# Four result tiles stored with one transfer each instead of two, and the last copy shared by two engines

## The chip, the cores and the metric

The kernel runs on one core of a Trainium2 chip. A core has a matrix engine (TensorE, PE in the profile), two engines that can read its accumulators in PSUM (VectorE, DVE in the profile, and ScalarE, ACT), GpSimd (POOL), and SyncE (SP), which here issues nearly all transfers between the chip's memory (HBM) and the on-chip buffer (SBUF). Transfers are carried out by 16 DMA engines. The metric is the device time of one execution in microseconds (us); less is better.

## The reference

Three layers follow each other, all in float32. First a delta-rule attention over 4 batches, 8 heads, 768 tokens and head size 48; then a feed-forward layer with a squared ReLU (384 to 2048 to 384); then a gated one (384 to 1536 to 384), whose result is what the kernel returns.

```python
for t in range(S):
    kt, vt, bt = (k_n[:, :, t], v[:, :, t], beta[:, :, t, None])
    y[:, :, t] = np.einsum('bhd,bhde->bhe', q[:, :, t], state)
    v_old = np.einsum('bhde,bhd->bhe', state, kt)
    state = state + bt[:, :, :, None] * np.einsum('bhd,bhe->bhde', kt, vt - v_old)
...
x = attn_out.transpose(0, 2, 1, 3).reshape(B * S, H * D)   # 3072 tokens x 384
h = np.maximum(x @ w_in, 0.0); x = h * h @ w_out
gate = 1.0 / (1.0 + np.exp(-(x @ w_gate)))
return gate * (x @ w_val) @ w_out                          # 3072 x 384
```

The rows of the result are ordered by batch: row b x 768 + t is token t of batch b.

## The kernel before, in words

Tokens are cut into 12 steps of 64 (`C`), and two steps of all four batches make a group of 512 columns (`GT`); there are six groups (`NG`). The attention and the first feed-forward layer run interleaved in an order that is written out by hand (`ORDER`); the change is not there. After that order is through, the second feed-forward layer runs group by group in a plain loop: for each of 72 values of n (6 groups by 12 slices of the hidden layer) `moe2_h(n)` makes gate and value and `moe2_o(n - 1)` multiplies the slice before by the output weights. Each matrix product is done as three, since both factors are split into a high and a low part.

In five groups `moe2_ot` does the output. In the last group `moe2_o` turns the product around: the 128 x 128 piece m of the activations is the stationary operand, so the accumulator `po2[m]` holds 128 tokens by 384 outputs. Piece m holds step s = 2g + m // 2 of two batches, b0 = 2 (m % 2) and b0 + 1, 64 tokens each. In the very last call (f = 11) the matmuls of m = 0, 1, 2, 3 follow each other (L930), and after those of each m its accumulator is copied to an SBUF tile `ob`, by VectorE for odd m (L939) and by ScalarE for even m (L941), and stored in two transfers on SyncE's queue (L945), one for each batch: 64 partitions of `ob` to 64 consecutive rows of the result. The tiles `ob` have four buffers, so no copy waits for a store. The copies also put the columns in order: in `o_in` and `o_out` the 384 columns are seen as q, m, i with sizes 4, 3, 32.

SyncE issues in the order of the program and waits in front of each store for the copy of its tile. After the last issue it waits for all transfers to land, and a closing exchange among the engines ends the program (L1041).

Of the kernel before, what the change touches and what calls it, by code (L numbers as in the profile page):

```python
# [15 lines left out]
NB, NH, SEQ, HD = 4, 8, 768, 48  # L16
DM, FF1, FF2 = 384, 2048, 1536
C = 64
# [64 lines left out]
def kernel(  # L83
# [20 lines left out]
    nc = tc.nc  # L104
# [655 lines left out]
    with tc.manual_schedule():  # L760
# [124 lines left out]
        def moe2_ot(n):  # L885

            g, f = divmod(n, NF2)
            if f == 0:
                po2[:KD] = [ps_o.tile([128, GT], F32, tag=f"o{m}", name=f"o{m}") for m in range(KD)]
            hi, lo = (w[:, 2 * DM:3 * DM] for w in w2_t[f])  # L890
            ph, pl = p_t.pop(n)
            for m in range(KD):
                for i, (w, x) in enumerate([(hi, ph), (lo, ph), (hi, pl)]):
                    nc.tensor.matmul(  # L894
                        out=po2[m], lhsT=w[:, m * 128:m * 128 + 128], rhs=x,
                        start=(f == 0 and i == 0), stop=(f == NF2 - 1 and i == 2),
                    )
            if f == NF2 - 1:

                ob = obt.tile([128, 16, KD * 32], F32, tag="obt", name="obt")  # L900
                for m in range(KD):
                    nc.vector.transpose(
                        out=ob[:, :, 32 * m:32 * m + 32], in_=po2[m].rearrange("p (t i) -> p t i", i=32)
                    )
                for s in range(2):
                    for b in range(NB):
                        r0 = b * SEQ + (2 * g + s) * C
                        for q in range(4):
                            nc.sync.dma_start(
                                out=out[r0:r0 + C, 96 * q:96 * q + 96].rearrange("(h i) d -> i h d", h=2),  # L910
                                in_=ob[quad(q), 8 * s + 2 * b:8 * s + 2 * b + 2],
                            )

        def moe2_o(n):
            g, f = divmod(n, NF2)
            if g < NG - 1:
                moe2_ot(n)
                return
            if f == 0:
                po2[:] = [  # L920
                    ps_o.tile([128, DM], F32, tag=f"o{m}", name=f"o{m}") if m < 3
                    else ps_2.tile([128, DM], F32, tag="o3", name="o3", bufs=1)
                    for m in range(4)
                ]
            hi, lo = (w[:, 2 * DM:3 * DM] for w in w2_t[f])
            ph, pl = p_t.pop(n)
            for m in range(4):
                cs = slice(m * 128, m * 128 + 128)
                for i, (x, w) in enumerate([(ph, hi), (ph, lo), (pl, hi)]):
                    nc.tensor.matmul(  # L930
                        out=po2[m], lhsT=x[:, cs], rhs=w,
                        start=(f == 0 and i == 0), stop=(f == NF2 - 1 and i == 2),
                    )
                if f == NF2 - 1:
                    ob = obp.tile([128, DM], F32, tag="ob", name="ob")
                    o_out = ob.rearrange("p (q m i) -> p m q i", q=4, m=KD)
                    o_in = po2[m].rearrange("p (m q i) -> p m q i", q=4, m=KD)
                    if m % 2:
                        nc.vector.tensor_copy(out=o_out, in_=o_in)  # L939
                    else:  # L940
                        nc.scalar.copy(out=o_out, in_=o_in)  # L941
                    s = 2 * g + m // 2
                    for b in range(2):
                        r0 = (2 * (m % 2) + b) * SEQ + s * C
                        nc.sync.dma_start(out=out[r0:r0 + C, :], in_=ob[64 * b:64 * b + 64])  # L945

        N2 = NG * NF2
        for n in range(N2 + 1):
            if n < N2:
                moe2_h(n)  # L950
                w2_split(n < 2)
                w2_late(n)
                g, f = divmod(n, NF2)
                if f == 2 and g + 1 < NG:
                    load_x2(g + 1)
                if 6 <= f < 9 and g + 1 < NG:
                    split_x2(g + 1, f - 6)
            w2_load()
            if n >= 1:
                moe2_o(n - 1)  # L960
# [84 lines left out]
```

## Time and profile before

| | us |
|---|---|
| median of 3 runs (1120.75 to 1122.94) | 1121.29 |
| span of the profiled execution, first to last instruction | 1116.7 |
| median less span: what lies around the span | 4.6 |
| TensorE busy | 1041.1 (93%) |
| VectorE busy | 584.0 (52%) |
| ScalarE busy | 428.8 (38%) |

The span is that of one execution under the profiler; no time of its own is listed for it, so the median of the runs less the span stands for what lies around it. TensorE's busy share says how full the engine is over the whole; at the very end of the program, where no matmul is left, other rows have to be read: when the copies ran, when the stores were issued, when their packets moved, and when the last one landed.

### The profile page before, as it was taken

The numbers are of one execution on the slowest core, as the hardware profiler recorded it, in microseconds if no ns is written. First come the engines' busy times: TensorE is split into PE (matmuls) and PEld (weight loads), VectorE is DVE, ScalarE is ACT, GpSimd is POOL, SyncE is SP. The second block draws the span as 40 slices with busy tenths as digits, with TensorE's granted clock in tenths as the row PEclk, the third lists the DMA queues.
The fourth block names the chain that finished last, engine by engine and source line by source line (L and its number), as shares of the span: only waits on it lengthen the run. The fifth ranks groups of instructions, "written<-read, shape, count | busy, mean of one in ns | idle before, by whom it ended". The sixth has DMA issues, their size and how long they took to land.

```text
span 1116.7 us, 27013 instructions
## 1 busy us (share of the span) xinstructions
PE 1041.1 (93%) x11764; PEld 862.7 (77%) x11770; DVE 584.0 (52%) x1099; ACT 428.8 (38%) x688; POOL 151.4 (14%) x117
## 2 busy tenths in 40 slices
PE   3486699899999999999999999999999999999997
PEld 3474578687887787788888888888888888888886
DVE  6659869785586798479433256632231222222222
ACT  2244374444447356345555564322212212222111
POOL 5123454200002001101100020200100001000000
PEclk9998689899999999999999999999999999999999
DMA  9428746566568758666645554101010020010101
GB/s 270 125 82 212 250 146 178 164 194 155 129 187 261 204 175 227 157 176 201 167 155 170 164 207 164 45 9 49 1 29 29 0 57 1 16 41 1 29 1 29
DMA packets 93030, 135.56 MB, mean 121 GB/s; under 512 B 45552, under 2 KB 72304, under 8 KB 92400
## 3 DMA queue, kind: packets, MB, share of 16 engines
q1 hardware_dynamic: 92624, 133.57, 41.2%
q8 instruction: 92, 1.51, 0.6%
q10 hardware_dynamic: 288, 0.26, 0.1%
q14 instruction: 26, 0.21, 0.1%
HBM read 108.63 MB, written 20.45 MB: 116 GB/s over the span
## 4 chain that ended last, share of the span: by engine, by line
PE 87%; DVE 5%; issue 3%; DMA 2%; POOL 1%; ACT 1%; SPq 0%; DVEq 0%; POOLq 0%
PE gv L868 26%; PE o L704 18%; PE h L666 17%; PE o L894 11%; PE o L930 2%; PE att L583 2%; PE att L540 1%; PE att L525 1%; PE att L571 1%; PE att L605 1%; DMA w1s<-in_w_dram 1%; PE att L553 1%; PE att L352 1%; PE h L740 1%; DVE tt L441 1%
## 5 line engine op out<-in xcount | busy, mean ns | idle before, releaser
L876 DVE TENSOR_TENSOR p<-sg,gv 128x512 f32<-128x512 f32 x72 | 49.5, 688 | 252.6 <-PE gv L868 252.6
L680 ACT ACTIVATE gg<-h 128x512 f32<-128x512 f32 x96 | 57.4, 598 | 195.6 <-PE h L666 186.1
L868 PE MATMUL gv<-xhi,w2h 128*128 128x512 f32 x432 | 121.5, 389 | 0.0
L868 PE MATMUL gv<-xlo,w2h 128*128 128x512 f32 x432 | 121.4, 389 | 0.0
L868 PE MATMUL gv<-xhi,w2l 128*128 128x512 f32 x432 | 121.4, 389 | 0.0
L704 PE MATMUL o<-gh,il 128*128 128x512 f32 x288 | 115.0, 399 | 0.0
L874 ACT ACTIVATE sg<-gv 128x512 f32<-128x512 f32 x72 | 43.2, 600 | 172.5 <-PE gv L868 172.5
L878 ACT CAST ph<-p 128x512 fp32r<-128x512 f32 x72 | 44.8, 622 | 156.5 <-DVE p L876 156.5
L689 DVE TENSOR_TENSOR gl<-gg,gh 128x512 fp32r<-128x512 f32 x96 | 72.1, 755 | 54.2 <-ACT gg L683 54.0
L868 PEld LDWEIGHTS gv<-xhi,w2l 128*128 128x128 f32 x432 | 81.1, 188 | 17.0
L868 PEld LDWEIGHTS gv<-xlo,w2h 128*128 128x128 f32 x432 | 81.1, 188 | 16.9
L868 PEld LDWEIGHTS gv<-xhi,w2h 128*128 128x128 f32 x432 | 81.0, 188 | 16.2
L704 PE MATMUL o<-gl,w1h 128*128 128x512 f32 x216 | 87.2, 404 | 5.0 <-DVE gl L689 4.9
L704 PE MATMUL o<-gh,w1h 128*128 128x512 f32 x216 | 90.6, 419 | 0.0
L666 PE MATMUL h<-xhi,il 128*128 128x512 f32 x288 | 83.1, 397 | 2.2 <-DMA il<-w1d 2.2
L880 DVE TENSOR_TENSOR pl<-p,ph 128x512 fp32r<-128x512 f32 x72 | 50.7, 704 | 49.5 <-ACT ph L878 49.5
L159 POOL TENSOR_TENSOR y<-raw 128x768 f32<-128x768 f32 (+1 forms) x16 | 27.9, 1743 | 314.4 <-DVE raw L152 248.4
L117 POOL TENSOR_TENSOR xlo<-x2r,xhi 128x512 fp32r<-128x512 f32 x18 | 24.7, 1370 | 336.8 <-ACT xhi L116 336.8
L894 PE MATMUL o<-ph,w2h 128*128 128x512 f32 x180 | 70.0, 389 | 0.0
L894 PE MATMUL o<-ph,w2l 128*128 128x512 f32 x180 | 70.0, 389 | 0.0
L894 PE MATMUL o<-pl,w2h 128*128 128x512 f32 x180 | 70.0, 389 | 0.0
L666 PE MATMUL h<-xhi,w1h 128*128 128x512 f32 x216 | 65.7, 413 | 3.5 <-ACT xhi L116 3.5
(144 smaller groups left out, 1898.6 us busy)
## 6 DMA issues: line engine op xcount, KB each, us to landing
il<-w1d SPq DMA_DIRECT2D x192, 192.0 KB, 3.3
raw<-in_w_dram SPq DMA_DIRECT2D x19, 768.0 KB, 6.1
w1s<-in_w_dram SPq DMA_DIRECT2D x9, 768.0 KB, 5.0
w1d<-wl SPq DMA_DIRECT2D x16, 384.0 KB, 4.7
kz<-in_kz_dram SPq DMA_DIRECT2D x32, 192.0 KB, 4.7
kn<-in_kn_dram SPq DMA_DIRECT2D x12, 384.0 KB, 4.8
kt<-in_kq_dram SPq DMA_DIRECT2D x24, 192.0 KB, 5.2
q<-in_kq_dram SPq DMA_DIRECT2D x24, 192.0 KB, 4.7
```

Source lines behind the costliest of these rows:

```text
L117: eng.tensor_tensor(out=dst_lo, in0=src, in1=dst_hi.bitcast(F32), op=ALU.subtract)
L159: nc.gpsimd.tensor_tensor(out=t, in0=c["t"], in1=c["raw"][:, :, 0].bitcast(F32), op=ALU.add)
L666: nc.tensor.matmul(out=ps[:, cs], lhsT=w[:, kc * 128:kc * 128 + 128], rhs=x[:, kc, cs], start=(i == 0 and kc == 0), stop=(i == 2 and kc == ...
L680: nc.scalar.activation(out=gg, in_=ps, func=ACTF.Relu)
L689: nc.vector.tensor_tensor(out=gl, in0=gg, in1=gh.bitcast(F32), op=ALU.subtract)
L704: nc.tensor.matmul(out=po[m], lhsT=w[:, cs], rhs=x, start=(f == 0 and i == 0), stop=(f == NF1 - 1 and i == 2),)
L868: nc.tensor.matmul(out=ps, lhsT=w[:, kc * 128:kc * 128 + 128], rhs=x[:, kc, :], start=(i == 0 and kc == 0), stop=(i == 2 and kc == KD - 1),)
L874: nc.scalar.activation(out=sg, in_=pss[0], func=ACTF.Sigmoid)
L876: nc.vector.tensor_tensor(out=p, in0=sg, in1=pss[1], op=ALU.mult)
L878: nc.scalar.copy(out=ph, in_=p)
L880: nc.vector.tensor_tensor(out=pl, in0=p, in1=ph.bitcast(F32), op=ALU.subtract)
L894: nc.tensor.matmul(out=po2[m], lhsT=w[:, m * 128:m * 128 + 128], rhs=x, start=(f == 0 and i == 0), stop=(f == NF2 - 1 and i == 2),)
```

## The change

Where the last call of `moe2_o` had two stores for each tile, it has one: its source is the whole tile of 128 partitions, its destination a pattern of three levels, 2 batches (768 rows apart) by 64 rows by 384 columns. And the copy of the tile m = 3, which VectorE did alone, is cut in two: q = 0, 1 (192 columns) on VectorE, q = 2, 3 (192 columns) on ScalarE.

```diff
-                    if m % 2:
+                    if m == 3:
+                        nc.vector.tensor_copy(out=o_out[:, :, 0:2], in_=o_in[:, :, 0:2])
+                        nc.scalar.copy(out=o_out[:, :, 2:4], in_=o_in[:, :, 2:4])
+                    elif m % 2:
                         nc.vector.tensor_copy(out=o_out, in_=o_in)
                     else:
                         nc.scalar.copy(out=o_out, in_=o_in)
                     s = 2 * g + m // 2
-                    for b in range(2):
-                        r0 = (2 * (m % 2) + b) * SEQ + s * C
-                        nc.sync.dma_start(out=out[r0:r0 + C, :], in_=ob[64 * b:64 * b + 64])
+                    b0 = 2 * (m % 2)
+                    nc.sync.dma_start(out=out.rearrange("(b s) d -> b s d", b=NB)[b0:b0 + 2, s * C:s * C + C, :], in_=ob)
```

On SyncE's queue the end of the program reads as follows, before (-) and now (+). L909 stores the results of the group before the last; a name in brackets is the counter that an instruction waits for (`DMAHW` a transfer's, `Activation` ScalarE's, `DVE` VectorE's).

```order
 L909 DMA out_dram<-obt 32x2x96 [waits DMAHW6_49]
-L945 DMA out_dram<-ob 64x384 [waits DMAHW7_49,Activation_49]
-L945 DMA out_dram<-ob 64x384 [waits DMAHW0_49]
-L945 DMA out_dram<-ob 64x384 [waits DMAHW1_49,DVE_49]
-L945 DMA out_dram<-ob 64x384 [waits DMAHW2_49]
-L945 DMA out_dram<-ob 64x384 [waits DMAHW3_49,Activation_49]
-L945 DMA out_dram<-ob 64x384 [waits DMAHW4_49]
-L945 DMA out_dram<-ob 64x384 [waits DMAHW5_49,DVE_49]
-L945 DMA out_dram<-ob 64x384 [waits DMAHW6_49]
-L1041 UNCONDITIONAL_BRANCH
+L947 DMA out_dram<-ob 2x64x384 [waits DMAHW7_49,Activation_49]
+L947 DMA out_dram<-ob 2x64x384 [waits DMAHW0_49,DVE_49]
+L947 DMA out_dram<-ob 2x64x384 [waits DMAHW1_49,Activation_49]
+L947 DMA out_dram<-ob 2x64x384 [waits DMAHW2_49,Activation_49]
+L1043 UNCONDITIONAL_BRANCH
```

Eight stores of 64 rows have become four whose destination has an outermost dimension of 2, and the last one waits for ScalarE.

On ScalarE the end of the program now reads (`o_11624`, `o_11626` and `o_11627` are the accumulators of m = 0, 2 and 3):

```order
669 L878 CAST ph<-p 128x512 [waits DVE_49]
670 L944 COPY ob<-o_11624 128x3x4x32 [waits PE_49]
671 L944 COPY ob<-o_11626 128x3x4x32 [waits PE_49]
672 L940 COPY ob<-o_11627 128x3x2x32 [waits DVE_49]
673 L1043 UNCONDITIONAL_BRANCH
```

The added copy stands behind the two that were there, and what it waits for is VectorE's counter: VectorE's own half of the same tile comes first.

## Rows read from the trace of the kernel before

**Rows 1.** Chain that ended last, its final pieces: start us, us, what.

```profile
1101.52 4.12 PE gv L868 x18
1105.64 4.28 PE o L930 x24
1109.92 0.02 issue
1109.94 0.56 DVE ob L939
```

**Rows 2.** Timeline of the end: start us, us, engine, line, operation.

```profile
1108.35 0.48 ACT L941 COPY ob<-o 128x384 f32<-128x384 f32 x1 [1.26 <-PE o L930]
...
1108.86 5.03 SPq L945 DMA_DIRECT2D out_dram<-ob  x8
...
1108.88 0.56 DVE L939 COPY ob<-o 128x384 f32<-128x384 f32 x1 [1.06 <-PE o L930]
...
1109.42 0.48 ACT L941 COPY ob<-o 128x384 f32<-128x384 f32 x1 [0.58 <-PE o L930]
...
1109.94 0.56 DVE L939 COPY ob<-o 128x384 f32<-128x384 f32 x1 [0.51 <-PE o L930]
```

**Rows 3.** The stores at L945: issue ns min/median/max, first and last start; us to landing.

```profile
L945 SPq DMA_DIRECT2D out_dram<-ob x8: 540/572/602, 1108.9 to 1113.3; - x8
...
DMA to landing us min/median/max: 2.1/2.2/2.2
```

**Rows 4.** DMA from 1110.0 to 1115.2 us: busy tenths in 40 slices, packets, queue.

```profile
DMA  3987149971599605897159950699306993069930
...
DMA packets 640, 0.79 MB, mean 151 GB/s; under 512 B 128, under 2 KB 640, under 8 KB 640
...
q1 hardware_dynamic: 640, 0.79, 63.6%
```

**Rows 5.** DMA from 660.0 to 662.5 us: one load of 128 rows of 1536 B.

```profile
DMA packets 144, 0.20 MB, mean 79 GB/s; under 512 B 16, under 2 KB 144, under 8 KB 144
...
q1 hardware_dynamic: 144, 0.20, 24.5%
```

**Rows 6.** DMA from 667 to 670 us: a store of 128 partitions, packets of 4096 B.

```profile
DMA packets 121, 0.50 MB, mean 165 GB/s; under 512 B 0, under 2 KB 0, under 8 KB 121
...
q1 hardware_dynamic: 121, 0.50, 41.5%
```

**Rows 7.** Costliest groups on the page, two of VectorE and ScalarE with 512 columns.

```profile
L876 DVE TENSOR_TENSOR p<-sg,gv 128x512 f32<-128x512 f32 x72 | 49.5, 688 | 252.6 <-PE gv L868 252.6
...
L874 ACT ACTIVATE sg<-gv 128x512 f32<-128x512 f32 x72 | 43.2, 600 | 172.5 <-PE gv L868 172.5
```

**Rows 8.** The loads at L644, 192 KB each: issue ns, and us to landing.

```profile
L644 SPq DMA_DIRECT2D il<-w1d x192: 319/382/4881, 39.8 to 659.7; - x192
...
DMA to landing us min/median/max: 2.3/3.3/8.1
```

## The prediction

> **What bounds the end now.** I read the chain that ended last first. Its final pieces [rows 1] are TensorE's 24 output matmuls, up to 1109.92 us, and VectorE's copy of the last tile, up to 1110.50. The span ends at 1116.7, so 6.2 us pass behind the last computing instruction, and all that the change touches lies there or just ahead of it. The timeline of the end [rows 2] shows what fills them: SyncE issues stores from 1108.86 for 5.03 us, while the four copies are done by 1110.50. The rows on the stores [rows 3] say that one issue takes 572 ns and that a store lands 2.2 us after its issue starts: the last issue, at 1113.3, lands at 1115.5, and 1.2 us later the program is over. So the eight issues in a row set the end, not the bytes. The DMA view of the same stretch [rows 4] shows it: busy digits rise and fall eight times, with gaps, from about 1110.05 to 1115.15, at 63.6% of the 16 engines. Each store moves when it is issued, and the next is not there yet.
>
> **How a store is dealt out.** The same rows [rows 4] count 640 packets, 128 of them under 512 B. The eight stores have 8 x 64 = 512 rows of 1536 B; the other 128 are 16 small ones for each store, one for each share. So each store of 64 rows went out in 16 shares of four rows. The one load of 128 rows [rows 5] has 128 + 16 packets: 16 shares of eight rows. In both, the outermost dimension of the transfer's pattern (64, 128) divides by 16.
>
> The new store's pattern on the result's side is 2 x 64 x 384, as the order of the instructions shows: outermost dimension 2. If shares are made along that dimension, there are two of them, 64 rows each, and two engines carry everything while 14 stand idle. If they are made by rows, whatever the levels of the pattern, there are 16 of eight rows. No transfer of before has an outermost dimension below 16, so the trace decides it neither way; I take two shares, since a share must be given a start and a count on both sides, and a single division of the outermost count is all that the transfers of this kernel ever needed.
>
> On this the Trainium skill has a rule (DMA: Bandwidth & Descriptors, section Rules for kernel authors): the number of DMA engines follows from each side's slowest dimension larger than 1, so an outermost dimension of c below 16 confines the whole transfer to c engines at most. By that rule the new stores run on two engines; no run here shows it yet.
>
> **The cost part by part.**
>
> *Four issues fewer.* Four times 572 ns [rows 3], 2.3 us of SyncE, on the path today. This is a gain only if the queue of issues stays the last thing that is waited for.
>
> *The stores' bytes on two engines.* Four stores of 64 packets for each engine are 256 packets in a row, since the second store is issued 0.6 us behind the first, long before the first is through. The price of a packet of 1536 B comes from three rows:
> - the stores of before: 63.6% of 16 engines over 5.2 us is 52.9 us of engine time, by 512 rows 103 ns [rows 4]. There 16 engines share 64 partitions;
> - the load of 128 rows: 24.5% of 16 x 2.5 us is 9.8 us, by 128 rows 77 ns [rows 5];
> - a store from 128 partitions with larger packets: 41.5% of 16 x 3 us is 19.9 us, by 121 packets 165 ns for 4096 B, by bytes 62 ns for 1536 B [rows 6].
>
> The new store reads all 128 partitions, and two engines get less in each other's way than 16, so I take a value by the third row, 67 ns, a little above it since packets are smaller. Then 256 x 0.067 = 17.2 us, against 5.1 us in which data move now. The first issue stays at 1108.86 (its copy is not changed), so data start at 1110.05 as today and end at 1127.2 instead of 1115.15: 12.1 us later. What follows (the landing of the last bytes, then 1.2 us of closing) stays. At 62 ns it would be 10.8 us later, at 77 ns 14.6, at 103 ns 21.3. Less than 62 ns is open too, because no row shows two engines alone.
>
> The skill's figure for one engine, about 27 GiB/s (same page, section Specifications), would make it 13.6 us for the 393 KB of each engine, an estimate, and a time near 1130 us; the row on the larger store, 24.8 GB/s, is slower than that.
>
> *The shared copy.* The last accumulator is ready at 1109.92. VectorE takes 558 ns for 384 columns [rows 2] and 688 for 512 [rows 7], about 1.02 ns a column, so 363 ns for 192; ScalarE 481 and 600 [rows 2, 7], 0.93 ns a column, so 303 ns. Side by side this would be done at 1110.30. But ScalarE's half waits for VectorE's counter, so they follow each other: 0.36 + 0.30 and some hundredths for the hand-over, ready at about 1110.67 instead of 1110.50. The split makes the copy 0.17 us later, not earlier. Nothing is queued behind it on ScalarE; SyncE's fourth issue waits for it. With two engines it costs nothing: at 1110.67 they are still in the first store (1110.05 to 1114.3), and the cover is over 12 us. Without that cover it is on the path, since SyncE comes free for the fourth issue at about the same moment.
>
> *Sum.* 1116.7 + 12.1 = 1128.8 us for the span; with the 4.6 us by which the median of the runs exceeds the span, 1133.4 us, 1.1% slower.
>
> **Rivals.**
>
> *All 16 engines carry the new store (the other side).* Then the issues bound the end as they do now, with four of them. They start at 1108.86, 1109.5 (behind the copy of m = 1, ready at 1109.44), 1110.1 and, behind the shared copy, 1110.75. A transfer of 192 KB lands at best 2.3 us after its issue [rows 8], so the last at 1113.05 instead of 1115.5; span 1114.25, time 1118.9, 0.2% faster. For it: issues are what is late now, and rows dealt out evenly are what all transfers of before show. Against it: the outermost dimension of 2. It decides from eight shares up: at 17.2 us of work for two engines, eight need 4.3 us and the issues bound again. The skill's advice on two transfers for disjoint halves of the partitions (same page, section Rules for kernel authors: they serialize, one of 128 partitions is better) speaks for this rival.
>
> *Two engines at the price of today's stores.* If 103 ns is what a packet from SBUF to the result costs in itself and not by 16 engines crowding 64 partitions, data need 26.4 us and the time is 1142.6. For it: same rows, same destination, same size [rows 4]. Against: the larger store is also from SBUF to HBM and costs 62 ns for as many bytes [rows 6].
>
> *Two engines, faster than any row.* With 14 engines silent a packet could fall to about 55 ns: 14.1 us, 9.0 us later, 1130.3. No row shows it.
>
> **How the numbers follow.** Two engines near 67 ns (62 to 77): 0.72, 1132.1 to 1135.9. Two engines towards 103 ns: 0.13. Two engines below 62 ns: 0.05. All 16 engines: 0.10. The range, 1130 to 1143 us, takes in all cases of two engines and leaves out the last. A change within 0.2% (2.2 us, about what a measurement of this kernel can tell from none) comes only from the last case, whose 2.4 us of gain lies on that bound: I give it 0.06 for faster and 0.04 for the same; slower 0.90.
>
> **What would show it.** Right: the span ends near 1129, data move without a gap from about 1110 to 1127, the DMA view of that stretch shows near 2 of 16 engines (12.5%) busy, and a store has two small closing packets, so 520 packets in all; the fourth store lands about 16 us after its issue. The third copy of ScalarE starts just behind VectorE's half, and the fourth issue stands near 1110.7. Wrong: 16 closing packets for each store with landings of 2 to 3 us (the 16-engine rival), or two engines with packets of 100 ns or more. If the issue itself grew, because two shares of 64 rows took longer to write out than 16 of eight, issues would be later, but that would hide behind the data unless it came to over 4 us each.

## The result, and the profile after

| | before | after |
|---|---|---|
| median, us (6 runs each) | 1121.9 | 1134.7 |
| ratio, 95% interval | | 1.0117 (1.0088 to 1.0147) |
| span of the profiled execution, us | 1116.7 | 1130.1 |
| last matmul ends, us | 1109.92 | 1111.43 |
| from there to the end of the span, us | 6.8 | 18.7 |

The changed kernel is 1.2% slower, 12.8 us by the medians. The profile puts it behind the last matmul: that stretch grew by 11.9 us, which lies in the interval of the ratio (9.9 to 16.5 us). The last matmul itself ended 1.5 us later in this execution, but the kernels run the same program up to there; among the further kernels below it ended anywhere from 1106.7 to 1116.4 us. So from here on the stretch behind the last matmul is compared, which repeats well: the two kernels with four merged stores gave 18.7 us each, and the two with the eight plain stores of before 6.8 each.

The chain that ended last, changed kernel; columns as in [rows 1]:

```profile
1107.18 4.25 PE o L930 x24
1111.43 0.02 issue
1111.45 0.37 DVE ob L939
1111.83 0.02 issue
1111.85 0.32 ACT ob L940
```

The shared copy is two copies in a row, ready 0.74 us after the last matmul, where before one copy took 0.58 [rows 1]. Behind it 18 us follow in which no engine computes. SyncE's waits say what for (engine and line, what it waited for: us in total, times, longest):

```profile
SPq L1043 <- DMA out_dram<-ob: 11.7, 1, 11.7
...
SPq L947 <- ACT ob L940: 0.4, 1, 0.4
```

One wait of 11.7 us for the stores to land; the wait for ScalarE's half is 0.4. The stores' issues (ns, min/median/max) and the DMA view from 1110 to 1130 us answer to [rows 3] and [rows 4]:

```profile
L947 SPq DMA_DIRECT2D out_dram<-ob x4: 538/1274/3208, 1110.4 to 1113.8; - x4
```

```profile
DMA  0001011101111111111111111111111111111000
...
DMA packets 520, 0.79 MB, mean 39 GB/s; under 512 B 8, under 2 KB 520, under 8 KB 520
...
q1 hardware_dynamic: 520, 0.79, 11.1%
```

The bytes are the same 0.79 MB, but the gaps between stores are gone and the busy digit is 1 for most of 17 us: 11.1% of 16 engines over 20 us is 35.5 us of engine time, two engines for 17.8 us. And 8 small packets for four stores are two for each. The same view of four quiet microseconds, 1120 to 1124, gives the price:

```profile
DMA packets 132, 0.20 MB, mean 50 GB/s; under 512 B 2, under 2 KB 132, under 8 KB 132
...
q1 hardware_dynamic: 132, 0.20, 13.2%
```

130 data packets in 4 us by two engines are one in 61.5 ns for each engine, with both of them always busy (two of 16 would be 12.5%; it is a little more because the recorded times of neighbouring packets overlap: 13.2% is 64 ns a packet).

### The profile page after: what moved, and what is told of

Read it like the earlier page. It is cut to its first block, busy times and chain, and to the rows that moved or that the text cites. A ratio compares the mean times of both kernels' runs of the same rounds, so it can differ in the third digit from the quotient of the medians.

```text
span 1130.1 us, 27016 instructions
## 1 busy us (share of the span) xinstructions
PE 1042.9 (92%) x11770; PEld 862.1 (76%) x11770; DVE 584.0 (52%) x1099; ACT 428.6 (38%) x689; POOL 150.9 (13%) x117
## 4 chain that ended last, share of the span: by engine, by line
PE 82%; DVE 4%; issue 3%; ACT 1%; POOL 1%; DMA 0%; ACTq 0%; SPq 0%; DVEq 0%; POOLq 0%
PE gv L868 26%; PE o L704 17%; PE h L666 16%; PE o L894 11%; PE o L930 2%; PE att L583 2%; PE att L571 1%; PE att L540 1%; PE att L605 1%; PE h L740 1%; PE att L352 1%; PE att L553 1%; PE att L525 1%; PE att L607 1%; PE att L366 1%
```

## The experiments

In each the time that counts is the stretch from the last matmul's end (in the chain) to the end of the span. Where no ratio is given, the kernel ran once, and the stretch is that of this one profiled execution.

**The merged stores alone** (the copy of m = 3 whole on VectorE, as before):

```diff
-                    if m == 3:
-                        nc.vector.tensor_copy(out=o_out[:, :, 0:2], in_=o_in[:, :, 0:2])
-                        nc.scalar.copy(out=o_out[:, :, 2:4], in_=o_in[:, :, 2:4])
-                    elif m % 2:
+                    if m % 2:
```

> Merged stores alone, the last copy whole on VectorE. Theory (two engines carry each merged store, the copy is hidden behind them): same as with both parts, about 1134 us, ratio to before 1.011 to 1.013; from the last matmul's end to the span's end 18.5 us (before 6.8, with both parts 18.7), 520 packets of which 8 are closing ones. Rival (the delay comes from ScalarE's half waiting for VectorE's, which puts the last store late): the time falls back to before, 1122 us, and the stretch behind the last matmul to 4 to 7 us.

Measured: ratio 1.0092 (1.0066 to 1.0118), median 1132.9 us. The final pieces of its chain:

```profile
1106.82 4.27 PE o L930 x24
1111.09 0.02 issue
1111.12 0.56 DVE ob L939
```

Its span is 1129.8, so 18.7 us lie behind the last matmul, as with both parts. The stores alone make the loss. The ratio came out below the range written down, with an interval that overlaps that of the full change.

**The shared copy alone** (stores in two, as before; the diff is the first half of the change's).

> The shared copy alone, stores in two as before. Theory: the copy ends 0.17 to 0.2 us later, but the seventh issue, which waits for it, starts only 2 us after that, so 0.0 us: ratio 0.998 to 1.002, stretch behind the last matmul 6.8 us. Rival (the split is what costs or what gains): the stretch changes by 0.2 us or more.

Measured: ratio 0.9999 (0.9967 to 1.0032), 6.8 us behind the last matmul. The chain shows the copy just as late as in the changed kernel, and the time doesn't see it (the span ends at 1119.8):

```profile
1108.74 4.25 PE o L930 x24
...
1113.01 0.37 DVE ob L939
1113.38 0.02 issue
1113.40 0.32 ACT ob L940
```

The half ready last is done at 1113.72; the issue that waits for it comes seventh, at 1115.80.

**The outermost dimension varied.** Eight stores of 64 rows as before, but with the result's side as x by 64/x by 384, for x = 4, 16 and 8:

```diff
-nc.sync.dma_start(out=out[r0:r0 + C, :], in_=ob[64 * b:64 * b + 64])
+nc.sync.dma_start(out=out[r0:r0 + C, :].rearrange("(y x) d -> x y d", x=4), in_=ob[64 * b:64 * b + 64])
```

> Eight stores as before, but the 64 rows of each go out as a pattern of 4 x 16 x 384 on the result's side, which puts the rows of a block of 64 in another order (rows r, r + 4, ...). Theory (a transfer is divided along its outermost dimension, here into four shares): 4 closing packets a store, 544 packets in all; each of four engines has 128 packets of 65 ns, 8.3 us and some more at the start, instead of 5.1 us, so the stretch behind the last matmul becomes 10 to 11 us (before 6.8), 3.3 to 4.2 us slower. Rival A (rows are dealt to 16 engines whatever the levels, and the change was slow for another reason): 640 packets, 6.8 us. Rival B (any pattern of three levels falls back to two engines): 528 packets, some 18.5 us.

> As the variant with 4 x 16 x 384, but 16 x 4 x 384 (the rows of a block of 64 in another order): a pattern of three levels whose outermost dimension is 16. Theory (shares along the outermost dimension): 16 closing packets a store, 640 packets, stretch behind the last matmul 6.8 us as before. Rival (three levels as such cost): 10 us or more.

> The same with 8 x 8 x 384 (rows in another order). Theory: 8 closing packets a store, 576 packets; eight engines have 64 packets each, 4.2 us, less than the issues take, so the stretch behind the last matmul is 6.6 to 7.3 us. The data packets should take 65 ns, not the 107 ns of before, if those come from 16 engines on 64 partitions at once; if a store from 64 partitions costs that much in itself, 107 ns and 6.9 us of data, 8 us or more.

For each of x = 4, x = 8 and x = 16, in this order, TensorE's last piece of the chain and the DMA view of the stores' stretch (1110.5 to 1122 us, 1115 to 1122, 1114.5 to 1119.7). The spans end at 1122.3, 1122.7 and 1121.1:

```profile
1106.49 4.27 PE o L930 x24
...
DMA packets 544, 0.79 MB, mean 68 GB/s; under 512 B 32, under 2 KB 544, under 8 KB 544
...
q1 hardware_dynamic: 544, 0.79, 21.6%
```

```profile
1110.88 4.25 PE o L930 x24
...
DMA packets 576, 0.79 MB, mean 112 GB/s; under 512 B 64, under 2 KB 576, under 8 KB 576
...
q1 hardware_dynamic: 576, 0.79, 36.8%
```

```profile
1110.10 4.25 PE o L930 x24
...
DMA packets 640, 0.79 MB, mean 151 GB/s; under 512 B 128, under 2 KB 640, under 8 KB 640
...
q1 hardware_dynamic: 640, 0.79, 43.7%
```

| outermost dimension | small packets a store | behind the last matmul, us |
|---|---|---|
| 64 (before) | 16 | 6.8 |
| 16 | 16 | 6.8 |
| 8 | 8 | 7.6 |
| 4 | 4 | 11.5 |
| 2 (after, four stores) | 2 | 18.7 |

At the three values tried below 16 the number of shares is the outermost dimension itself, and with 4 and 2 the stretch grows with the packets that one engine gets. With 8 about 0.5 of the 0.8 us comes from the issues: they took 604 ns at the median instead of 572, and the last began 3.9 us behind the last matmul instead of 3.4. A pattern of three levels as such costs nothing (16 x 4). The sizes for 4 and 8 came out 0.5 and 0.3 us above what I had written down: for x = 4 the engine time, 21.6% of 16 engines over 11.5 us, is 78 ns for each of 512 packets instead of 65, and for x = 8, 36.8% over 7 us, it is 80. These are means: in the packet records of the traces the median data packet took 65 ns for x = 4, 8 and 16 and in the changed kernel, and 107 ns in the kernel before; longer ones raise the means (up to 584 ns for x = 4, 173 for x = 8).

**The last tile alone merged.**

```diff
+                    if m == 3:
+                        nc.sync.dma_start(out=out.rearrange("(b s) d -> b s d", b=NB)[2:4, s * C:s * C + C, :], in_=ob)
+                        continue
                     for b in range(2):
```

> Only the last tile's two stores are merged into one of 2 x 64 x 384, the other six stay. Theory: its issue is the seventh, 2.8 us after the last matmul, its 64 packets for each of two engines take 4.2 us from 1.2 us after that; with 0.35 us to land and 1.2 us to close the stretch behind the last matmul is 9.7 us, 2.9 us slower than before. 512 data and 6 x 16 + 2 = 98 closing packets. Rival (the cost comes from several merged stores waiting for each other in the queue): 7 us or less.

Measured: 98 small packets; the last matmul ended at 1116.39 and the span at 1126.8, so 10.4 us, 0.7 more than expected. The DMA view from 1116 to 1126.8 us shows both kinds of store one behind the other, first six on 16 engines, then one on two:

```profile
1112.14 4.25 PE o L930 x24
...
DMA  0086582946839385111101011111111111000000
...
DMA packets 610, 0.79 MB, mean 73 GB/s; under 512 B 98, under 2 KB 610, under 8 KB 610
```

One merged store, with nothing behind it, already costs 3.6 us: the loss doesn't need several of them in the queue. Four in a row then add up, since they share the same two engines. The 0.7 us more are a slow start: from 1120.6 to 1122.8 us, when its issue was over, 45 data packets moved where the rate of 61.5 ns an engine gives 72.

**All 16 engines, one store a tile.** The columns of the last group's input are put in another order when it is split, so that piece m of the activations holds 128 consecutive rows of batch m:

```diff
+            hi, lo, src = x2[g][0][:, kc], x2[g][1][:, kc], x2r[g][:, kc]
+            if g == NG - 1:
+                hi, lo = (t.rearrange("p (b s c) -> p b s c", b=NB, s=2) for t in (hi, lo))
+                src = src.rearrange("p (s b c) -> p b s c", b=NB, s=2)
+            split(hi, lo, src, nc.gpsimd)
...
-                    for b in range(2):
-                        r0 = (2 * (m % 2) + b) * SEQ + s * C
-                        nc.sync.dma_start(out=out[r0:r0 + C, :], in_=ob[64 * b:64 * b + 64])
+                    r0 = m * SEQ + 2 * g * C
+                    nc.sync.dma_start(out=out[r0:r0 + 2 * C, :], in_=ob)
```

> The columns of the last group's input are put in the order batch, step, token when the input is split, so that tile m holds 128 consecutive rows of batch m and is stored whole with a plain pattern of 128 x 384; copies as before. Theory (128 divides by 16, so all 16 engines carry it, and four issues bound the end no more): 64 closing packets, the last store is issued as its copy ends and lands 2.3 us later, the stretch behind the last matmul is 0.6 + 2.3 + 1.2 = 4.1 us instead of 6.8; 2.7 us faster, ratio 0.997 to 0.999, about 1119.3 us. Rival (a store of 192 KB is limited by bytes or rows, not by engines): no gain or a loss, 1122 us or more.

Measured: median 1115.9 us beside 1122.3 for before, ratio 0.9955 (0.9924 to 0.9986), the lowest ratio of all. Its chain ends with the whole copy on VectorE; its issues and landings, and the DMA view from 1106 to 1110 us:

```profile
1102.51 4.25 PE o L934 x24
1106.76 0.02 issue
1106.78 0.56 DVE ob L943
```

```profile
L947 SPq DMA_DIRECT2D out_dram<-ob x4: 332/350/397, 1105.7 to 1107.4; - x4
...
DMA to landing us min/median/max: 1.9/1.9/2.0
```

```profile
DMA  0000027999858999999999999998300000000000
...
DMA packets 576, 0.79 MB, mean 197 GB/s; under 512 B 64, under 2 KB 576, under 8 KB 576
...
q1 hardware_dynamic: 576, 0.79, 54.6%
```

The span is 1110.65, so 3.9 us behind the last matmul instead of 6.8: 2.9 us, or a ratio of 0.9974, are shown. The rest of the measured ratio is not: its profile has the last matmul 3 us earlier than that of before, but GpSimd's first split was as far ahead (645.0 us against 648.1) long before the last group's, which is the changed one (its last piece starts at 1011.7), and 0.9974 lies in the interval.

**The shared copy on top of that.** The kernel with whole stores of 128 rows, and the copy of m = 3 in two halves.

> The stores of 128 plain rows (16 engines) and the shared copy on top. Here nothing covers the copy: with plain stores the last issue starts as the last copy ends. Theory (ScalarE's half waits for VectorE's): the copy ends 0.71 us after the last matmul instead of 0.60, so the stretch behind the last matmul is 4.0 to 4.1 us (3.9 with the whole copy on VectorE): 0.1 to 0.2 us slower than without the split, which the times cannot tell; ratio to before 0.995 to 0.999. Rival (the halves run side by side when the stores let them): 3.6 to 3.7 us.

Measured: ratio 0.9962 (0.9926 to 0.9998). The copies (durations ns, first and last start):

```profile
L946 DVE COPY ob<-o x1: 558/558/558, 1113.9 to 1113.9; 128x384 f32<-128x384 f32 x1
L943 DVE COPY ob<-o x1: 357/357/357, 1115.0 to 1115.0; 128x192 f32<-128x192 f32 x1
L944 ACT COPY ob<-o x1: 319/319/319, 1115.4 to 1115.4; 128x192 f32<-128x192 f32 x1
```

They follow each other here too. The chain has the last matmul's end at 1114.94 and the span ends at 1118.86, so 3.9 us: the split brings nothing where it could, and the 0.1 us that it should cost is not seen either.

**Why a packet took 103 ns before.** The variant with 16 x 4 x 384 has the same 16 engines, and the same 64 partitions as source, but 43.7% busy instead of 63.6% [rows 4]. Two kernels were to tell whether the distance of the engines' rows in the result decides. One stores 32 x 2 x 384 (x = 32 in the first diff on the outermost dimension), the other plain rows into every other row of a block of 128:

```diff
-                        r0 = (2 * (m % 2) + b) * SEQ + s * C
-                        nc.sync.dma_start(out=out[r0:r0 + C, :], in_=ob[64 * b:64 * b + 64])
+                        r0 = m * SEQ + 2 * g * C
+                        nc.sync.dma_start(out=out[r0:r0 + 2 * C, :].rearrange("(p e) d -> e p d", e=2)[b], in_=ob[64 * b:64 * b + 64])
```

> Why a data packet of the stores takes 107 ns before, and 65 ns in the variant with 16 x 4 x 384, which has the same 16 engines and the same source partitions. Here 32 x 2 x 384 (rows in another order): each engine has four packets, its first rows 3072 B from its neighbour's, where before they are 6144 B apart. Theory (the places of the 16 engines' rows in the result decide, 6144 B apart being a bad distance): 65 ns, busy share of the stores' stretch near 0.40 instead of 0.64. Rival (16 engines reading 64 partitions, and the variant was an exception): 107 ns. Either way 640 packets and a stretch behind the last matmul of 6.8 us.

> The same question. Stores of 64 plain rows from 64 partitions as before, but to every other row of a block of 128 (rows in another order): neighbouring engines' rows are 12288 B apart, rows of one engine 3072 B. Theory (6144 B apart is what costs): 65 ns, as in the stores of 128 plain rows, where engines are also 12288 B apart. Rival (16 engines on 64 partitions, each with rows one behind the other): 107 ns. 640 packets and a stretch behind the last matmul of 6.8 us either way.

The same 5.2 us of each in the DMA view, 32 x 2 first (from 1112.6 us), every other row second (from 1112.5):

```profile
q1 hardware_dynamic: 640, 0.79, 64.0%
```

```profile
q1 hardware_dynamic: 640, 0.79, 63.5%
```

Both have the price of before, 103 to 104 ns by 512 data packets (median 107), and 6.9 and 6.8 us behind the last matmul. My theory of the distance fell. Stores of 64 partitions on 16 engines cost this much in three layouts of the result out of four. In the fourth, 16 x 4, they are at 43.7% of 16 x 5.2 us by 512, 71 ns, and why it is spared stays open; so 16 engines on 64 partitions are not enough to explain the price. The stores on 128 partitions are at 54.6% of 16 x 4 us by 512, 68 ns.

## Why the prediction was right, point by point

The forecast was 1133.4 us, 12.1 us more than before; measured were 1134.7 us, 12.8 more by the medians, and 11.9 us in the stretch that the forecast was about. The mechanism was right; that its size came out within 0.2 us of that stretch is in part luck, as the price of a packet shows.

*Two shares.* This decided everything, and the trace of before could not show it, since all its transfers had outermost dimensions that divide by 16. Now it is shown, by two small packets a store, and by 4, 8 and 16 of them where the pattern was made so. The Trainium skill's rule (DMA: Bandwidth & Descriptors, section Rules for kernel authors: an outermost dimension below 16 confines a transfer to at most that many engines) agrees with the shares counted for 2, 4 and 8. The rival of 16 engines is out for this pattern, and its price was nearly right for the kernel that does reach 16 engines with four stores: 3.9 us behind the last matmul, where the rival's working gives 4.3.

*The price of a packet.* Taken as 67 ns, between the rows for 62 and 77, for one steady flow. In steady flow it is 61.5 ns, just below that range and close to the row of the larger store, but the first microseconds are slower, which the prediction didn't have. The DMA view from 1111.6 to 1114 us counts

```profile
DMA packets 48, 0.07 MB, mean 31 GB/s; under 512 B 0, under 2 KB 48, under 8 KB 48
```

48 packets where the steady rate gives 78. In sum 256 packets an engine from about 1111.7 to 1128.5 are 16.8 us, against the 17.2 forecast: 15.7 at the steady rate and 1 us of slow start. So two errors nearly cancelled, a price too high by 5.5 ns (1.4 us) and a start taken as steady. What makes the start slow stays open; here SyncE was still issuing, but with the last tile alone merged the start was as slow with no issue left. The rival of 103 ns a packet is refuted by the steady rate, and no run showed two engines below 61.5 ns, so the faster rival's 55 has nothing for it. The reason I gave, that 16 engines crowd 64 partitions, does not suffice: the variant with 16 x 4 had the same crowd and 71 ns.

*The issues.* I had the fourth issue 0.8 us after the last matmul and allowed for growth only as a possibility. It happened: the third issue took 1.9 us and the fourth 3.2, so the fourth began 2.35 us behind the last matmul (1113.78), and its store was waited for until 14.9 us after that, where I had said about 16. As foreseen, the stores that were still moving covered it. The four issues saved were worth nothing here. With 16 engines, fewer and shorter issues are nearly the whole gain: the last began 0.6 us behind the last matmul (1107.4) instead of 3.4, some 2.7 of the 2.9 us.

*The copies.* Foreseen as one behind the other, 363 and 303 ns, 0.17 us later in sum; measured 358 and 318 ns, 0.16 us later, and hidden.

*What lies around the span.* A step that was off without effect: I added 4.6 us, the median of before less its profiled span. The runs of the changed kernel list time and span together, and they differ by 1.7 us. The other 2.9 us, then, were a profiled execution of before quicker than the median. The difference of kernels was right because both sides carried the same term.

*The chances.* Slower had 0.90. The rival of 16 engines (0.10) was told apart by one row, the count of small packets, and that of 103 ns a packet (0.13) by the packets' rate in the quiet stretch.

## What to carry to other kernels

Merging transfers at the end of a program pays only if the merged pattern still has an outermost dimension that all DMA engines can share; here a 2 in front of 64 rows took 14 of 16 engines out, and 0.4 MB through one engine took 17 us. Arrange the data earlier so that the small dimension disappears: changing the order of columns in work that was done anyway gave one plain store a tile and 2.9 us off the end. With the small dimension inside (32 x 2) a store went out in 16 shares as well, but that run laid the rows in another order, so whether this can replace the merged store was not tried. At the end of a program, where nothing covers a transfer, count the small closing packets of a store in the DMA view; in all these runs they told into how many shares it was cut. And a copy split over two engines is shared only if the second half doesn't wait for the first: look at its wait before counting on it.

## What the runs showed of the hardware that was not expected

A store of 192 KB from 128 partitions lands 1.9 us after its issue starts, one of 96 KB from 64 partitions after 2.2 [rows 3], and the issue of the larger takes 350 ns against 572: twice the bytes in less time.

An issue is not always short: behind two and then three stores still moving on two engines it took 1.9 and then 3.2 us, and with four engines the seventh of eight took 1.4. Whether SyncE waits for room in a queue was not tried.

Each of two engines carried 1536 B in 61.5 ns, 25.0 GB/s. The Trainium skill's figure for one engine (DMA: Bandwidth & Descriptors, section Specifications), about 27 GiB/s, which is 29 GB/s, was not reached.
